# A fused attention and max-FFN kernel: later transposes go from TensorE to the DMA queue, the exp table is loaded first, and two FFN chunks are interleaved

## The chip, the cores and the metric

The kernel runs on one core of a Trainium2 chip. The metric is the device time of one execution in microseconds (us); the times below are medians over runs, and the profile is that of one further execution. In the profile the engines are PE (TensorE; PEld is its weight load), DVE (VectorE), ACT (ScalarE), POOL (GpSimd) and SP (SyncE), which here issues every DMA.

## The reference

Local attention with a few global keys feeds a feed-forward layer that takes the larger of three products:

```python
scores = scale * q @ k.T                      # (4, 8, 768, 768), head size 64
keep = (key < 8) | (0 <= query - key < 96)
scores = where(keep, scores - slope[h] * dist, -1e9)   # dist is 96 for the 8 global keys
a = softmax(scores)
x = (a @ v).transpose(0, 2, 1, 3).reshape(3072, 512)
h = max(x @ w1, x @ w2, x @ w3)               # 512 -> 768
out = h @ w_out                               # 768 -> 512
```

Inputs and output are float32; the kernel multiplies in bfloat16.

## The kernel before

The 3072 rows are cut into 24 tiles of 128, six for each of the four batches. A query tile needs its own keys, those of the tile before it and eight global keys, so that a tile's scores are two blocks of 128 keys per head. The global keys and values overwrite the first eight rows of the preceding tile's block (units G and V).

All work is written as units, and the string `SCHEDULE` names them in one order. Each engine runs its part of the units strictly in that order; waits between engines are semaphores that the framework adds. The units that matter here, with T a tile and g one of two groups of four heads:

- **L**T loads q, k and v of tile T (three DMAs of 256 KB, line 145). The last of six `raw` buffers must have been read before the load.
- **C**T.0 casts q and k to bfloat16 (`qkb`), C T.1 casts v. The last number picks the engine: 0 ACT, 1 DVE, 2 POOL, 3 half DVE and half POOL.
- **X**T turns q and k (128 rows by 1024 columns) by eight TensorE transposes (line 197) into PSUM and copies the result to `qkT` (lines 199, 200, 202).
- **S**T.g computes scores in PSUM (line 220) and ACT takes their exponential into P (line 225). A last number of 1 adds distance and mask first, by two more matmuls with `bias` (line 211); with 0, unit **M** multiplies P by `wmask` on DVE afterwards.
- **A**T.g multiplies P with v (lines 257 and 260), and DVE divides by the row sum into `xb` (lines 266 and 267).
- **T**T turns the 128 by 512 result `xb` by four TensorE transposes (line 284) and copies it to `xT` (line 285).
- **F**c.f.j is one FFN block of chunk c: four matmuls (line 296) for f of six column blocks and weight j of three; j = 0 is copied by ACT, the others are maxed in by DVE. The chunks hold 4, 2, 2, 4, 4, 4, 4 tiles, and a chunk's F units need T of all its tiles.
- **O**c.t is the second product for one tile (six matmuls, line 311), a copy and a store. **E** does this for the last chunk.
- **w**, **o** load FFN weights (512 KB each), **W**, **Q** cast them. **B** makes `bias` (line 232) and **K** makes `wmask` (line 237) for one head, both from the table of distances `rbase`.

Both X and T hold a second branch with `dma_start_transpose` on SP, reached before only for T of 99 or more, so never.

PSUM gives three buffers to FFN blocks and products (`psH`), one to transposes (`psT`), and one to each group's scores and attention product (`psS`).

Of the kernel before, what the change touches and what calls it, by code (L numbers as in the profile page):

```python
# [22 lines left out]


SCHEDULE = """
    L1 B0.1 B1.2 K0 K1 K2 K3 L2 K4 B2.2 C0.0.1 B3.2 B4.1 B5.2 X0.1 K5 K6 L3 S0.0.1 w0.0 B6.2 B7.2 S0.1.1
    G0.2 C1.0.3 X1.0 C2.0.2 C3.0.2 C0.1.1 C1.1.1 C2.1.2 M0.0 K7 M0.1 A0.0 A0.1 S1.0.1 M1.0 T0.0 S1.1.1
    A1.0 X2.3 G1.0 M1.1 A1.1 S2.0.1 L4 M2.0 w0.1 S2.1.1 T1.1 w0.2 X3.3 V1.2 A2.0 L5 M2.1 W0.0.2 C3.1.0
    A2.1 C4.0.3 G2.0 S3.0.1 S3.1.1 V2.2 T2.1 X4.3 M3.0 A3.0 M3.1 A3.1 T3.1 V3.1 G3.0 S4.0.1 W0.1.1
    S4.1.0 w1.0 G4.0 w1.1 C4.1.1 W0.2.2 F0.0.0 C5.0.2 M4.0 M4.1 F0.0.1 A4.0 A4.1 F0.0.2 X5.3 W1.0.1  # L30
    C5.1.2 F0.1.0 T4.0 W1.1.1 F0.1.1 F0.1.2 F0.2.0 V4.1 w1.2 W1.2.2 L6 w2.0 W2.0.2 C6.1.2 S5.0.0 S5.1.1
    w2.1 M5.0 F0.2.1 F0.2.2 C6.0.0 A5.0 F0.3.0 w2.2 X6.0 F0.3.1 M5.1 A5.1 S6.0.1 F0.3.2 M6.0 L7 S6.1.1
    T5.0 A6.0 W2.2.1 F0.4.0 o1 W2.1.2 L8 M6.1 A6.1 G6.0 F0.4.1 o0 o2 C7.0.2 Q1.2 F0.4.2 F0.5.0 C7.1.1
    F0.5.1 F0.5.2 C8.0.3 F1.0.0 X7.0 F1.0.1 F1.0.2 F1.1.0 L9 S7.0.0 S7.1.0 F1.1.1 F1.1.2 F1.2.0 L10 X8.0
    C8.1.0 M7.0 M7.1 F1.2.1 F1.2.2 L11 F1.3.0 G7.2 A7.0 A7.1 Q0.0 T6.1 Q2.2 L12 F1.3.1 F1.3.2 F1.4.0
    S8.0.0 S8.1.0 M8.0 T7.0 V7.1 O0.0.0 O0.1.0 C9.0.1 X9.0 M8.1 A8.0 A8.1 G8.2 F1.4.1 L13 F1.4.2 F1.5.0
    C10.0.2 T8.1 C9.1.1 C10.1.1 S9.0.0 S9.1.0 M9.0 M9.1 G9.1 O0.2.0 X10.0 F1.5.1 L14 C11.0.0 V8.1
    C12.0.2 O0.3.0 C11.1.2 A9.0 A9.1 F1.5.2 F2.0.0 X11.3 L15 S10.0.0 S10.1.0 F2.0.1 F2.0.2 C12.1.0 G10.1
    O1.0.0 M10.0 F2.1.0 M10.1 T9.0 V9.2 A10.0 F2.1.1 F2.1.2 F2.2.0 A10.1 X12.1 C13.0.2 S11.0.0 S11.1.0
    F2.2.1 O1.1.0 M11.0 M11.1 T10.0 V10.2 A11.0 F2.2.2 F2.3.0 F2.3.1 C13.1.2 A11.1 F2.3.2 X13.3 S12.0.0  # L40
    S12.1.0 F2.4.0 M12.0 M12.1 F2.4.1 F2.4.2 C14.0.0 A12.0 T11.0 F2.5.0 A12.1 F2.5.1 F2.5.2 X14.3 G12.0
    S13.0.0 M13.0 S13.1.0 F3.0.0 L16 C14.1.0 M13.1 G13.0 F3.0.1 F3.0.2 A13.0 A13.1 T12.1 F3.1.0 V13.2
    F3.1.1 C15.0.3 S14.0.0 S14.1.0 G14.0 L17 M14.0 O2.0.1 M14.1 F3.1.2 F3.2.0 C15.1.1 C16.1.1 X15.3
    A14.0 A14.1 F3.2.1 F3.2.2 T13.0 F3.3.0 L18 S15.0.0 S15.1.0 V14.1 M15.0 M15.1 C16.0.2 X16.0 F3.3.1
    O2.1.0 A15.0 A15.1 L19 L20 F3.3.2 G15.2 T14.0 C17.0.3 C18.0.1 C17.1.1 F3.4.0 S16.0.0 S16.1.0 X17.1
    V15.1 L21 L22 F3.4.1 F3.4.2 T15.0 M16.0 F3.5.0 F3.5.1 M16.1 F3.5.2 X18.0 F4.0.0 A16.0 G16.1 A16.1
    F4.0.1 F4.0.2 F4.1.0 C18.1.0 F4.1.1 S17.0.0 S17.1.0 C19.1.1 C19.0.3 C20.0.3 M17.0 L23 M17.1 V16.2
    F4.1.2 F4.2.0 F4.2.1 X19.0 A17.0 A17.1 F4.2.2 F4.3.0 F4.3.1 S18.0.0 M18.0 S18.1.0 G18.0 M18.1 O3.0.1
    O3.1.0 C21.0.3 A18.0 A18.1 X20.0 C22.0.0 C23.0.3 F4.3.2 F4.4.0 F4.4.1 S19.0.0 M19.0 S19.1.0 M19.1
    G19.2 T16.0 F4.4.2 F4.5.0 F4.5.1 A19.0 T17.0 A19.1 V19.2 C20.1.2 O3.2.1 T18.0 F4.5.2 T19.0 S20.0.0  # L50
    M20.0 S20.1.0 M20.1 O3.3.0 X21.3 F5.0.0 F5.0.1 O4.0.0 A20.0 G20.2 A20.1 V20.2 O4.1.0 S21.0.0 S21.1.0
    T20.1 M21.0 F5.0.2 X22.0 G21.1 F5.1.0 F5.1.1 F5.1.2 C21.1.0 A21.0 F5.2.0 F5.2.1 C22.1.2 F5.2.2
    F5.3.0 M21.1 F5.3.1 F5.3.2 A21.1 F5.4.0 F5.4.1 S22.0.0 S22.1.0 C23.1.2 T21.1 M22.0 F5.4.2 V21.2
    M22.1 F5.5.0 F5.5.1 X23.0 F5.5.2 A22.0 A22.1 G22.0 O4.2.0 S23.0.0 S23.1.0 T22.0 O4.3.0 O5.0.0 M23.0
    V22.2 M23.1 O5.1.0 A23.0 A23.1 O5.2.1 T23.0 O5.3.1 F6.0.0 F6.0.1 F6.0.2 F6.1.0 F6.1.1 F6.1.2 F6.2.0
    F6.2.1 F6.2.2 F6.3.0 F6.3.1 F6.3.2 F6.4.0 F6.4.1 F6.4.2 F6.5.0 F6.5.1 F6.5.2 E
"""


# [1 line left out]
def kernel(  # L61
# [77 lines left out]
    def load(T):  # L139
        b, t = divmod(T, NT)  # L140
        r = raw_pool.tile([128, 3, H, D], FP32, name="raw", tag="raw")
        raw[T] = r
        sl = slice(t * 128, (t + 1) * 128)
        for i, src in enumerate((q, k, v)):
            nc.sync.dma_start(out=r[:, i], in_=src[b, :, sl, :].rearrange("h s d -> s h d"))
# [33 lines left out]
    def early(T):  # L179
        return T < NSTART  # L180

    def u_X(T, how):
        if T >= 99:
            qkT[T] = qkT_pool.tile([128, 2, NP, 128], BF16, name="qkT", tag="qkT")
            nc.sync.dma_start_transpose(out=qkT[T].rearrange("p a j s -> p (a j) s"),
                                        in_=qb[T].rearrange("p a c -> p (a c)"))
            return
        qkT[T] = qkT_pool.tile([128, 2, NP, 128], BF16, name="qkT", tag="qkT")
        if how == 3:
            tps = [psT.tile([128, NP, 128], BF16, name="tp", tag="tp"),  # L190
                   psH.tile([128, NP, 128], BF16, name="tpk", tag="h")]
        else:
            tp = psT.tile([128, 2, NP, 128], BF16, name="tp", tag="tp")
            tps = [tp[:, a] for a in range(2)]
        for a in range(2):
            for jp in range(NP):
                nc.tensor.transpose(tps[a][:, jp], qb[T][:, a, jp * 128:(jp + 1) * 128], identb)  # L197
        if how == 3:
            nc.scalar.copy(qkT[T][:, 0], tps[0])
            nc.vector.tensor_copy(qkT[T][:, 1], tps[1])  # L200
        else:
            copies[how](qkT[T], tp)  # L202
# [25 lines left out]
    def u_B(h, how):  # L228
        g, hp = divmod(h, 4)
        j2, hh = divmod(hp, 2)  # L230
        eng = (None, nc.vector, nc.gpsimd)[how]
        eng.tensor_scalar_mul(bias[:, g, hh, j2], rbase, -slopes[h] / scale)  # L232
# [37 lines left out]
    def u_XT(T, how):  # L270
        c, i = where[T]
        if i == 0:
            xT[c] = xT_pool.tile([128, NP, len(chunks[c]) * 128], BF16, name="xT", tag="xT")
# [8 lines left out]
        x = xb[T].rearrange("p h d -> p (h d)")
        for jp in range(NP):
            nc.tensor.transpose(tp[:, jp], x[:, jp * 128:(jp + 1) * 128], identb)  # L284
        copies[how](xT[c][:, :, i * 128:(i + 1) * 128], tp)  # L285
# [85 lines left out]
    with tc.manual_schedule():  # L371
        load(0)

        make_identity(nc, identf)
# [23 lines left out]
        nc.vector.tensor_scalar_min(rbase[0:NG, 2, :], rbase[0:NG, 2, :], float(NL))  # L398
# [39 lines left out]
```

## Time and profile before

| | before |
|---|---|
| time, median of 3 runs | 195.0 us (194.93 to 195.02) |
| profiled execution | 194.84 us |
| its span (first to last instruction) | 193.1 us |
| instructions recorded | 4284 |
| read from and written to memory | 25.17 MB, 6.29 MB |
| DMA packets, of these under 512 B | 84068, 75472 |

The span starts with the first instruction that the profiler records; 1.7 us of the execution lie outside it. The packets under 512 B are those of q, k and v: a row of one head is 64 float32, 256 bytes.

### The profile page before, as it was taken

To read this page: it belongs to the slowest core of one execution; us is meant where nothing else is said; L and a number is where in the kernel's file an instruction comes from. 1 tells how busy PE (TensorE), PEld (TensorE's weight loads), DVE (VectorE), ACT (ScalarE), POOL (GpSimd) and SP (SyncE) were. 2 spreads that over 40 slices of the span, in tenths; PEclk is the share of its full clock that TensorE was granted. 3 is DMA by queue.
4 is the path that set the end of the run, shared out by engine and by line. 5 is a ranking of instruction groups with operands and counts; after the bars stand their busy time and mean duration, and the time that the engine had idled before them with its cause. 6 is when DMAs were issued, how large, how long until landed. Compare 5 with 4: busy or idle time off the path is not lost.

```text
span 193.1 us, 4284 instructions
## 1 busy us (share of the span) xinstructions
PE 178.1 (92%) x1670; PEld 103.6 (54%) x1670; DVE 124.7 (65%) x291; ACT 112.0 (58%) x176; POOL 41.1 (21%) x66
## 2 busy tenths in 40 slices
PE   0459988999999999999999999999999999999993
PEld 0236455454786678775555555555554455544442
DVE  3632577668596857878969869668555776345520
ACT  2736665664589786695567446485765276422221
POOL 6973422352320144004010230011030000000000
PEclk9999999999999999999999999999999999999999
DMA  7999999999898999999365999420220001420005
GB/s 144 218 218 259 286 213 347 237 305 259 211 257 181 233 277 232 254 262 200 100 121 139 234 218 205 98 93 3 109 112 0 2 0 58 163 109 0 3 0 217
DMA packets 84068, 31.73 MB, mean 164 GB/s; under 512 B 75472, under 2 KB 80336, under 8 KB 84048
## 3 DMA queue, kind: packets, MB, share of 16 engines
q1 hardware_dynamic: 84048, 31.46, 72.1%
q8 instruction: 13, 0.21, 0.5%
q14 instruction: 7, 0.06, 0.1%
HBM read 25.17 MB, written 6.29 MB: 163 GB/s over the span
## 4 chain that ended last, share of the span: by engine, by line
PE 88%; POOL 5%; DVE 4%; issue 1%; ACT 1%; POOLq 0%; DVEq 0%; ACTq 0%
PE h L296 48%; PE po L311 16%; PE sp L220 7%; PE tp L197 4%; POOL bias L232 4%; PE xtp L284 3%; PE sp L211 3%; PE op L257 3%; PE op L260 2%; DVE xb L267 1%; PE tpk L197 1%; ACT P L225 1%; DVE xT L285 0%; DVE qkT L200 0%; DVE rz L266 0%
## 5 line engine op out<-in xcount | busy, mean ns | idle before, releaser
L296 PE MATMUL h<-xT,w 128*128 128x512 bf16 (+1 forms) x504 | 101.8, 349 | 0.0
L296 PEld LDWEIGHTS <-w 128*128 128x128 bf16 x504 | 46.5, 98 | 37.5
L225 ACT ACTIVATE P<-sp 128x1024 bf16<-128x1024 f32 (+1 forms) x48 | 43.5, 953 | 13.3 <-PE sp L220 13.2
L301 ACT CAST h<-h 128x512 bf16<-128x512 f32 (+1 forms) x42 | 22.3, 531 | 34.9 <-PE h L296 33.7
L303 DVE TENSOR_TENSOR h<-h,h 128x512 bf16<-128x512 bf16 (+1 forms) x42 | 25.6, 609 | 19.9 <-PE h L296 19.7
L311 PE MATMUL po<-wo,ht 128*128 128x512 bf16 (+1 forms) x150 | 33.9, 371 | 0.0
L244 DVE TENSOR_TENSOR P<-P,wmask 128x1024 bf16<-128x1024 bf16 x32 | 21.9, 691 | 10.5 <-ACT P L225 10.4
L305 DVE TENSOR_TENSOR ht<-h,h 128x512 bf16<-128x512 bf16 (+1 forms) x42 | 25.6, 609 | 4.5 <-PE h L296 1.5
L267 DVE TENSOR_TENSOR xb<-op,rz 128x256 bf16<-128x256 f32 x48 | 20.4, 425 | 1.7
L311 PEld LDWEIGHTS <-ht 128*128 128x128 bf16 x150 | 13.9, 98 | 13.8
L197 PE MATMUL tp<-identb,qkb 128*128 128x128 bf16 x156 | 13.7, 231 | 6.2 <-DVE qkb L163 6.2
L197 PEld LDWEIGHTS <-qkb 128*128 128x128 bf16 x192 | 13.2, 104 | 9.4 <-DVE qkb L163 6.1
L317 ACT COPY ost<-po 128x512 f32<-128x512 f32 (+1 forms) x19 | 11.0, 582 | 11.3 <-PE po L311 10.7
L220 PEld LDWEIGHTS <-qkT 64*128 64x128 bf16 x352 | 10.2, 96 | 12.7 <-issue 7.8
L266 DVE RECIPROCAL rz<-op 128x4 f32<-128x4 f32 x48 | 8.5, 176 | 12.1 <-PE op L260 8.4
L220 PE MATMUL sp<-qkT 64*128 64x128 bf16 x352 | 16.0, 224 | 0.0
L257 PEld LDWEIGHTS <-P 128*128 128x128 bf16 x192 | 13.8, 100 | 3.5 <-DVE P L244 0.7
L257 PE MATMUL op<-va,P 128*128 128x65 bf16 x160 | 13.9, 195 | 0.9 <-DVE P L244 0.6
L202 ACT COPY qkT<-tp 128x1024 bf16<-128x1024 bf16 x12 | 12.2, 1021 | 3.8 <-PE tp L197 3.6
L285 ACT COPY xT<-xtp 128x512 bf16<-128x512 bf16 x16 | 9.5, 591 | 7.2 <-PE xtp L284 7.2
L163 POOL CAST qkb<-raw 128x1024 bf16<-128x1024 f32 x8 | 8.5, 1060 | 20.2 <-DMA raw<-in_k_dram 14.3
L177 POOL COPY va<-vaf 8x260 int32<-8x260 int32 x10 | 4.0, 398 | 40.5 <-PE op L260 40.5
(58 smaller groups left out, 140.9 us busy)
## 6 DMA issues: line engine op xcount, KB each, us to landing
raw<-in_q_dram SPq DMA_DIRECT2D x24, 256.0 KB, 5.1
raw<-in_k_dram SPq DMA_DIRECT2D x24, 256.0 KB, 5.2
raw<-in_v_dram SPq DMA_DIRECT2D x24, 256.0 KB, 5.2
out_dram<-ost SPq DMA_DIRECT2D x23, 256.0 KB, 2.1
wst<-in_moe_w_dram SPq DMA_DIRECT2D x9, 512.0 KB, 5.6
wst<-in_moe_w_out_dram SPq DMA_DIRECT2D x3, 512.0 KB, 6.1
out_dram<-ost SPq DMA_DIRECT2D x2, 128.0 KB, 1.9
```

Source lines behind the costliest of these rows:

```text
L197: nc.tensor.transpose(tps[a][:, jp], qb[T][:, a, jp * 128:(jp + 1) * 128], identb)
L202: copies[how](qkT[T], tp)
L220: nc.tensor.matmul(sp[:, hh, j2, ds], st, qkT[T][hsl, 0, jp], start=not how, stop=True, skip_group_check=True)
L225: nc.scalar.activation(P[:, :, 0:n], sp.rearrange("p a b d n -> p (a b) d n")[:, :, 0:n], AF.Exp, bias=0.0, scale=scale)
L244: nc.vector.tensor_mul(P, P, wmask[:, g, :, 0:2])
L257: nc.tensor.matmul(o, P[:, i, 0], heads(va[T])[:, h], start=True, stop=(t == 0), skip_group_check=True)
L267: nc.vector.tensor_tensor(out=x[:, 4 * g:4 * g + 4], in0=op[:, :, 0:64], in1=rz[:, :, None].to_broadcast([128, 4, D]), op=ALU.mult)
L296: nc.tensor.matmul(ps, w123[f // 2][:, dm, j, (f % 2) * 128:(f % 2) * 128 + 128], xT[c][:, dm], start=(dm == 0), stop=(dm == 3))
L301: nc.scalar.copy(h01, ps)
L303: nc.vector.tensor_max(h01s[c, f], h01s[c, f], ps)
L305: nc.vector.tensor_max(ht[c][:, f], h01s[c, f], ps)
L311: nc.tensor.matmul(po, ht[c][:, f, tt * 128:(tt + 1) * 128], wo[:, f, cols], start=(f == 0), stop=(f == NF - 1))
```

## The change

- `SCHEDULE` is another order of the same 486 units, with other engines for some. Ten of the 24 X units (tiles 13 to 15 and 17 to 23) and twelve of the 24 T units (tiles 9, 10, 12 to 14, 16 to 18 and 20 to 23) now end in 4: they take the branch with the DMA transpose, which SP issues in its queue between loads and stores.
- A 128 by 1 tile `tiny` is set to zero and put through the exponential ahead of everything else, so that ACT loads its exp table there.
- Unit B can go to ACT; of the eight, six are on DVE and two on ACT (before two on DVE and six on POOL).
- The first loads are six tiles (L0 to L5), then six FFN weights, where weights stood between tiles before. FFN blocks of chunk 0 (tiles 0 to 3) and chunk 1 (tiles 4 and 5) alternate; before, chunk 0 was finished first.
- Buffers: `cast` 3 to 4, `qkT` 4 to 5, `pp` 5 to 6.
- The exponentials with bias (last number of S is 1) are again twelve, now both groups of tiles 0 to 5.

```diff
 SCHEDULE = """
-    L1 B0.1 B1.2 K0 K1 K2 K3 L2 K4 B2.2 C0.0.1 B3.2 B4.1 B5.2 X0.1 K5 K6 L3 S0.0.1 w0.0 B6.2 B7.2 S0.1.1
+    K0 B0.1 C0.1.2 B1.1 B2.0 K1 K2 L1 B3.0 B4.1 K3 B5.1 B6.1 C0.0.1 X0.3 S0.0.1 M0.0 K4 K5 L2 B7.1
...
-    cast_pool = ctx.enter_context(tc.tile_pool(name="cast", bufs=3))
-    qkT_pool = ctx.enter_context(tc.tile_pool(name="qkT", bufs=4))
-    p_pool = ctx.enter_context(tc.tile_pool(name="pp", bufs=5))
+    cast_pool = ctx.enter_context(tc.tile_pool(name="cast", bufs=4))
+    qkT_pool = ctx.enter_context(tc.tile_pool(name="qkT", bufs=5))
+    p_pool = ctx.enter_context(tc.tile_pool(name="pp", bufs=6))
...
+    tiny = persist.tile([128, 1], FP32, name="tiny")
...
     def u_X(T, how):
-        if T >= 99:
+        if how == 4:
             qkT[T] = qkT_pool.tile([128, 2, NP, 128], BF16, name="qkT", tag="qkT")
             nc.sync.dma_start_transpose(out=qkT[T].rearrange("p a j s -> p (a j) s"),
                                         in_=qb[T].rearrange("p a c -> p (a c)"))
...
-        eng = (None, nc.vector, nc.gpsimd)[how]
-        eng.tensor_scalar_mul(bias[:, g, hh, j2], rbase, -slopes[h] / scale)
+        mul = (nc.scalar.mul, nc.vector.tensor_scalar_mul, nc.gpsimd.tensor_scalar_mul)[how]
+        mul(bias[:, g, hh, j2], rbase, -slopes[h] / scale)
...
-        if T >= 99:
+        if how == 4:
             nc.sync.dma_start_transpose(out=xT[c][:, :, i * 128:(i + 1) * 128],
                                         in_=xb[T].rearrange("p h d -> p (h d)"))
...
         load(0)
+
+        nc.vector.memset(tiny, 0.0)
+        nc.scalar.activation(tiny, tiny, AF.Exp, bias=0.0, scale=1.0)
```

**SP, the loads of the last tiles.** In the order before, from tile 19 on, SP issues nothing but loads here (three rows are one tile, `raw`):

```order
L145 DMA raw_1888<-in_q_dram 128x8x64
L145 DMA raw_1888<-in_k_dram 128x8x64
L145 DMA raw_1888<-in_v_dram 128x8x64
L145 DMA raw_1892<-in_q_dram 128x8x64
L145 DMA raw_1892<-in_k_dram 128x8x64
L145 DMA raw_1892<-in_v_dram 128x8x64
```

In the changed order, from the load of tile 19 to that of tile 20:

```order
L147 DMA raw_1998<-in_q_dram 128x8x64
L147 DMA raw_1998<-in_k_dram 128x8x64
L147 DMA raw_1998<-in_v_dram 128x8x64
L187 DMA_TRANSPOSE qkT_2026<-qkb_1955 128x8x128
L277 DMA_TRANSPOSE xT_2069<-xb_1967 128x4x128
L187 DMA_TRANSPOSE qkT_2112<-qkb_2002 128x8x128
L147 DMA raw_2121<-in_q_dram 128x8x64
L147 DMA raw_2121<-in_k_dram 128x8x64
L147 DMA raw_2121<-in_v_dram 128x8x64
```

Three transposes (q/k of tile 18, result of tile 16, q/k of tile 19) now stand between the two loads. The last reads `qkb`, a cast of the tile loaded three rows above it, so the load of tile 20 cannot be issued before tile 19 has arrived and been cast.

**ACT, the first instructions.** Before, the exp table is loaded by the first K, and no product of `bias` is on ACT:

```order
L237 ACT_TABLE_LOAD
L237 ACTIVATE wmask_103<-rbase_102 128x384 x7
L225 ACTIVATE P_195<-sp_188 128x4x128
L225 ACTIVATE P_208<-sp_201 128x4x128
L202 COPY qkT_214<-tp_215 128x1024
```

In the changed order:

```order
L377 ACT_TABLE_LOAD
L377 ACTIVATE tiny_102<-tiny_102 128x1
L239 ACTIVATE wmask_104<-rbase_103 128x384
L234 ACTIVATE bias_105<-rbase_103 128x384
L239 ACTIVATE wmask_104<-rbase_103 128x384 x2
L234 ACTIVATE bias_105<-rbase_103 128x384
L239 ACTIVATE wmask_104<-rbase_103 128x384
L201 COPY qkT_171<-tp_172 128x512
L227 ACTIVATE P_191<-sp_184 128x4x128
```

The table load has moved ahead of the wait for `rbase`, and two `bias` products stand among the first `wmask`; POOL has none left.

**ACT, where the FFN begins.** Before, the first copies of FFN blocks (`h01`) come after the exponentials of tile 4 (the first two rows); q/k of tile 5 and results of later tiles are copied between the blocks:

```order
L225 ACTIVATE P_501<-sp_490 128x1024
L225 ACTIVATE P_513<-sp_504 128x1024
L172 COPY qkT_444<-kg8_0_111 128x4x8
L301 CAST h01_528<-h_523 128x512
L199 COPY qkT_570<-tp_571 128x512
L301 CAST h01_590<-h_585 128x512
L285 COPY xT_592<-xtp_593 128x4x128
```

In the changed order they come after those of tile 5, and behind a weight cast on ACT (`w123`, unit W0.2):

```order
L227 ACTIVATE P_568<-sp_557 128x1024
L227 ACTIVATE P_581<-sp_570 128x1024
L287 COPY xT_583<-xtp_584 128x4x128
L362 CAST w123_0_114<-wst_591 128x4x256
L303 CAST h01_616<-h_611 128x512
```

The attention of one more tile lies ahead of the first FFN block, and the copy of that block waits behind the cast of a weight.

More of the change, by code (lines that the diff above doesn't have):

```diff
@@ L25 @@
 SCHEDULE = """
-    L1 B0.1 B1.2 K0 K1 K2 K3 L2 K4 B2.2 C0.0.1 B3.2 B4.1 B5.2 X0.1 K5 K6 L3 S0.0.1 w0.0 B6.2 B7.2 S0.1.1
[L27 to L55, printed above, removed]
@@ L56 @@
-    F6.2.1 F6.2.2 F6.3.0 F6.3.1 F6.3.2 F6.4.0 F6.4.1 F6.4.2 F6.5.0 F6.5.1 F6.5.2 E
+    K0 B0.1 C0.1.2 B1.1 B2.0 K1 K2 L1 B3.0 B4.1 K3 B5.1 B6.1 C0.0.1 X0.3 S0.0.1 M0.0 K4 K5 L2 B7.1
+    S0.1.1 K6 G0.0 C1.0.3 A0.0 C2.0.2 K7 X1.3 M0.1 A0.1 C1.1.0 C2.1.1 S1.0.1 S1.1.1 M1.0 L3 M1.1 A1.0
+    X2.3 A1.1 G1.0 V1.1 S2.0.1 M2.0 L4 S2.1.1 G2.0 A2.0 C3.0.2 M2.1 X3.3 L5 T0.0 A2.1 C4.0.1 S3.0.1
+    S3.1.1 T1.1 C3.1.2 V2.2 M3.0 M3.1 X4.0 A3.0 w0.0 A3.1 w0.1 G3.0 S4.0.1 S4.1.1 M4.0 M4.1 G4.2 C4.1.1
+    C5.0.1 V3.1 X5.0 T2.0 A4.0 A4.1 T3.1 S5.0.1 M5.0 S5.1.1 T4.0 M5.1 V4.2 w0.2 C5.1.2 W0.0.2 A5.0
@@ new lines @@
+    W0.1.2 W0.2.0 F0.0.0 A5.1 F0.0.1 T5.1 F0.0.2 F0.1.0 F0.1.1 w1.0 F0.1.2 F1.0.0 W1.0.2 F0.2.0 F1.0.1
+    F1.0.2 w1.2 F1.1.0 F1.1.1 w1.1 L6 W1.1.2 F1.1.2 F0.2.1 C6.0.0 F1.2.0 C6.1.1 F1.2.1 X6.1 W1.2.2
+    F1.2.2 L7 C7.0.0 F0.2.2 S6.0.0 S6.1.0 C7.1.0 M6.0 w2.2 F1.3.0 X7.0 w2.0 M6.1 W2.0.2 F1.3.1 A6.0
+    F0.3.0 w2.1 A6.1 L8 F0.3.1 G6.2 S7.0.0 S7.1.0 G7.1 C8.0.2 F1.3.2 F1.4.0 W2.1.0 M7.0 M7.1 F0.3.2
+    W2.2.0 L9 T6.1 o0 F0.4.0 C8.1.2 A7.0 A7.1 F0.4.1 X8.0 F0.4.2 F1.4.1 F1.4.2 S8.0.0 S8.1.0 T7.1 M8.0
@@ new lines @@
+    M8.1 F0.5.0 F1.5.0 F1.5.1 V7.2 o2 C9.0.2 G8.1 X9.0 o1 L10 A8.0 Q0.0 A8.1 F0.5.1 F0.5.2 Q2.2 L11
+    S9.0.0 S9.1.0 T8.0 C10.0.0 Q1.2 V8.2 F1.5.2 C9.1.2 O0.0.0 G9.2 M9.0 O0.1.0 M9.1 L12 C11.0.2 A9.0
+    X10.1 A9.1 V9.2 O0.2.0 S10.0.0 S10.1.0 G10.1 O0.3.0 T9.4 F2.0.0 C10.1.1 C11.1.0 M10.0 X11.0 C12.0.2
+    M10.1 F2.0.1 A10.0 A10.1 F2.0.2 V10.2 F2.1.0 F2.1.1 S11.0.0 S11.1.0 F2.1.2 F2.2.0 C12.1.0 M11.0
+    M11.1 F2.2.1 F2.2.2 T10.4 X12.1 L13 C13.0.2 A11.0 O1.0.0 A11.1 F2.3.0 L14 X13.4 F2.3.1 F2.3.2
@@ new lines @@
+    S12.0.0 S12.1.0 M12.0 M12.1 T11.1 F2.4.0 O1.1.0 F2.4.1 F2.4.2 F2.5.0 F2.5.1 F2.5.2 F3.0.0 A12.0
+    F3.0.1 A12.1 C14.0.2 L15 C13.1.2 F3.0.2 X14.4 G12.2 F3.1.0 C14.1.0 F3.1.1 S13.0.0 M13.0 S13.1.0
+    G13.1 L16 O2.0.0 M13.1 C15.0.1 F3.1.2 F3.2.0 A13.0 A13.1 F3.2.1 V13.2 F3.2.2 S14.0.0 X15.4 S14.1.0
+    G14.2 T12.4 M14.0 F3.3.0 C16.0.3 M14.1 F3.3.1 L17 F3.3.2 A14.0 F3.4.0 A14.1 V14.2 X16.3 F3.4.1 T13.4
+    S15.0.0 M15.0 S15.1.0 C15.1.2 O2.1.0 M15.1 F3.4.2 F3.5.0 A15.0 A15.1 F3.5.1 F3.5.2 T14.4 L18 C17.0.0
@@ new lines @@
+    C16.1.2 C17.1.2 G15.0 S16.0.0 M16.0 S16.1.0 X17.4 M16.1 T15.1 O3.0.0 O3.1.0 O3.2.1 F4.0.0 C18.0.1
+    V15.2 A16.0 C18.1.2 A16.1 V16.1 G16.2 F4.0.1 F4.0.2 L19 C19.0.2 S17.0.0 S17.1.0 X18.4 M17.0 M17.1
+    F4.1.0 F4.1.1 A17.0 F4.1.2 F4.2.0 T16.4 C19.1.2 A17.1 F4.2.1 F4.2.2 S18.0.0 M18.0 S18.1.0 M18.1
+    X19.4 F4.3.0 L20 L21 C20.0.0 T17.4 X20.4 G18.0 C20.1.2 F4.3.1 F4.3.2 A18.0 A18.1 T18.4 F4.4.0 F4.4.1
+    S19.0.0 S19.1.0 F4.4.2 M19.0 F4.5.0 M19.1 F4.5.1 C21.0.0 X21.4 L22 L23 F4.5.2 A19.0 A19.1 V19.2
@@ new lines @@
+    O3.3.0 O4.0.0 G19.1 T19.0 O4.1.1 S20.0.0 S20.1.0 F5.0.0 M20.0 M20.1 F5.0.1 G20.1 C22.0.0 F5.0.2
+    A20.0 F5.1.0 A20.1 V20.2 F5.1.1 F5.1.2 S21.0.0 S21.1.0 C21.1.2 M21.0 M21.1 C23.0.3 F5.2.0 G21.1
+    F5.2.1 F5.2.2 X22.4 F5.3.0 A21.0 A21.1 V21.2 F5.3.1 F5.3.2 S22.0.0 S22.1.0 M22.0 F5.4.0 M22.1 T20.4
+    T21.4 F5.4.1 C22.1.2 A22.0 G22.0 F5.4.2 F5.5.0 A22.1 X23.4 F5.5.1 F5.5.2 T22.4 S23.0.0 S23.1.0
+    O4.2.0 V22.1 C23.1.2 M23.0 M23.1 O4.3.1 A23.0 A23.1 T23.4 O5.0.0 O5.1.0 O5.2.0 O5.3.1 F6.0.0 F6.0.1
@@ L57 @@
+    F6.0.2 F6.1.0 F6.1.1 F6.1.2 F6.2.0 F6.2.1 F6.2.2 F6.3.0 F6.3.1 F6.3.2 F6.4.0 F6.4.1 F6.4.2 F6.5.0
+    F6.5.1 F6.5.2 E
 """
```

## The prediction, made before the changed kernel was run

> **What bounds the kernel now.** I read the page first: busy time, the span in 40 slices (4.83 us each) and the shares of the chain that ended last.
>
> ```profile
> PE 178.1 (92%) x1670; PEld 103.6 (54%) x1670; DVE 124.7 (65%) x291; ACT 112.0 (58%) x176; POOL 41.1 (21%) x66
> PE   0459988999999999999999999999999999999993
> DMA  7999999999898999999365999420220001420005
> GB/s 144 218 218 259 286 213 347 237 305 259 211 257 181 233 277 232 254 262 200 100 121 139 234 218 205 98 93 3 109 112 0 2 0 58 163 109 0 3 0 217
> PE 88%; POOL 5%; DVE 4%; issue 1%; ACT 1%; POOLq 0%; DVEq 0%; ACTq 0%
> ```
>
> PE is full from the eighth slice on, and the chain runs through it for 88% of the span. The rest of the chain is a start in which PE waits. The DMA engines are full until about 90 us and mostly free behind 120 us. So three things count: PE work, PE's idle time at the start, and whether loads keep pace in the first half. The stages, in the view of busy time by stretch (stretch, length, then busy us of each engine; at the end clock, DMA share, GB/s):
>
> ```profile
> 31.40:58.00 26.60, 26.59 (x257) 16.43 (x256) 19.73 (x46) 16.21 (x26) 8.13 (x9) 1.00 1.08 260
> 87.00:123.00 36.00, 35.97 (x335) 19.49 (x334) 29.48 (x66) 21.64 (x33) 5.29 (x9) 1.00 0.89 173
> 123.00:169.00 46.00, 46.00 (x402) 24.68 (x401) 29.14 (x62) 26.84 (x41) 4.31 (x10) 1.00 0.15 58
> ```
>
> PE has no gap to speak of in any of them, at full granted clock; no other engine passes 82%. But a busy PE is not PE's price for an instruction, since matmuls overlap. The price is the time between one group and the next in the chain of waits (start, length, what):
>
> ```profile
> 31.41 0.86 PE h L296 x4
> 50.12 0.45 PE tp L197 x8
> 52.05 0.55 PE sp L220 x16
> 54.47 1.31 PE h L296 x12
> 56.26 0.22 PE xtp L284 x4
> 66.57 1.29 PE po L311 x6
> 124.93 0.26 PE op L257 x8
> 19.34 0.43 PE sp L211 x2
> 184.55 5.21 PE po L311 x30
> 189.84 0.42 DVE ost L317
> ```
>
> So X on TensorE costs 0.45 us, T 0.22, an FFN block 0.86 (0.44 in a chunk of two tiles), a tile's scores 0.55 for both groups, `bias` 0.43 a group, an attention product 0.26, O 1.29. Over all units of the table this makes 168.5 us: FFN 93.3, O and E 31.0, X 10.8, T 5.3, scores and `bias` 16.7, attention 11.4. The last matmul ends at 189.8, so PE idles 21.3 us in all. Where?
>
> ```profile
> 3.73 1.28 ACT L237 ACT_TABLE_LOAD   x1 [3.73 <-DVE rbase L398]
> 3.83 4.99 POOL bias L232 x4
> 8.88 1.24 POOL bias L232
> 10.20 1.23 POOL bias L232
> 11.47 0.37 PE sp L211
> 12.21 0.60 ACT L225 ACTIVATE P<-sp 128x512 bf16<-128x512 f32 x1 [3.14 <-PE sp L220]
> 30.99 0.20 PE op L257
> ```
>
> Six `bias` products on POOL hold the second group of tile 0 until 11.47; ACT idles 3.14 us for it. From there tiles follow one another until 30.99, when the attention of tile 4 begins; behind that PE is full. Ahead of 30.99 PE has done X for five tiles (2.25), scores and `bias` of tiles 0 to 4 (5.9), attention of tiles 0 to 3 (1.8), four T (0.9) and two FFN blocks (1.7): 12.6 us. So **18.4 us of the idle time lie ahead of 30.99**, 2.9 behind it.
>
> **The change, part by part.** *Transposes leave PE.* Ten X by 0.45 and twelve T by 0.22 are 4.5 + 2.6 = **7.1 us** of PE work gone. All lie behind tile 9, where PE is full, so all of it counts if PE stays the bound. Their copies go too:
>
> ```profile
> L202 ACT COPY qkT<-tp 128x1024 bf16<-128x1024 bf16 x12 | 12.2, 1021 | 3.8 <-PE tp L197 3.6
> L285 ACT COPY xT<-xtp 128x512 bf16<-128x512 bf16 x16 | 9.5, 591 | 7.2 <-PE xtp L284 7.2
> ```
>
> ACT loses six of the first and eleven of the second kind, some 12 us; three more q/k casts and three weight casts there (1.07 each) give back 6. DVE sheds five splits of casts and copies. None of this was the bound: nothing is added for it.
>
> *What a DMA transpose costs* the trace does not show. Nearest rows:
>
> ```profile
> 113.31 1.14 SPq L145 DMA_DIRECT2D raw<-in_k_dram  x1
> 114.49 1.10 SPq L145 DMA_DIRECT2D raw<-in_v_dram  x1
> raw<-in_k_dram SPq DMA_DIRECT2D x24, 256.0 KB, 5.2
> out_dram<-ost SPq DMA_DIRECT2D x23, 256.0 KB, 2.1
> ```
>
> With the queue full, 256 KB in packets of 256 B (1024 of them, 64 per DMA engine) pass in 1.14 us; a store into a free queue has landed in 2.1. An X transpose is 256 KB whose contiguous block rows are 256 B too. Call its time in the queue c (T: half). From the load row by size of piece: c is 1.14 for 256 B, 2.3 for 128 B, 4.6 for 64 B, 9.1 for 32 B. Below, a queue that overlaps it wholly gives 0. I take 1.14, the load's row, as nearest in bytes and packets, and keep 0 to 9.1.
>
> What decides is the tightest stretch. It runs from the end of O3.2 (chunk 3's third product) to S of tile 22. In it PE has 30 FFN blocks (25.9), three O (3.9), scores of five tiles (2.75), six attentions (3.1) and a T (0.2): 35.9 us. Ahead of tile 22's transpose the queue carries, with it, 0.9 for the last store's copy, 15 loads by 1.14 (17.1), three stores by 0.9 (2.7), five X (5c) and three T (1.5c). 20.7 + 6.5c = 35.9 gives **c = 2.3**. Below that, transposes cost nothing; above, each us of c costs 6.5 us. Single steps also hold at c = 1.14: the last T has the four O of chunk 5 (5.2 us) ahead of chunk 6, against 0.8 for DVE, 0.6 in the queue and about 2 to land. SP waits in line here: each transpose waits for its cast or division, and the next tile's load stands behind it. Loads behind 123 us have a DMA share of 0.15 to fill, so later loads are bearable. I charge **0**; at c = 9.1 it is the last but one of the rivals.
>
> The Trainium skill speaks against this step: "VectorE: DVE Perf Modes", section "The three transpose paths", gives 1309 ns for a 128 by 128 DMA transpose and 390 ns on TensorE. Its TensorE figure does not agree with the 56 ns apiece of the chain (0.45 / 8); no run here shows its DMA figure. If eight blocks went one by one, c would be 10.5 (estimate from that page) and the sum as in the rival of the swamped queue. Its page "Advanced Engine Details and Errata", section "X-Bar Transpose (TRN2)", says the opposite, 350 to 400 GB/s, an estimated c of 0.7, with which the sum is my forecast.
>
> *The start.* `bias` goes to DVE and ACT, and ACT's table load hides in the wait for `rbase`:
>
> ```profile
> L232 DVE TENSOR_SCALAR bias<-rbase 128x384 bf16<-128x384 f32 x2 | 1.0, 503 | 0.0
> L225 ACT ACTIVATE P<-sp 128x1024 bf16<-128x1024 f32 x40 | 38.9, 1024 | 7.9 <-PE sp L220 7.8
> 16.09 1.04 POOL L163 CAST qkb<-raw 128x1024 bf16<-128x1024 f32 x1 [2.60 <-DMA raw<-in_k_dram]
> L363 ACT CAST wo<-wst 128x1024 bf16<-128x1024 f32 x1 | 1.1, 1078 | 0.0
> L301 ACT CAST h<-h 128x512 bf16<-128x512 f32 x30 | 17.7, 591 | 30.2 <-PE h L296 29.0 <-DVE ht L305 1.1
> ```
>
> Five products by 0.5 on DVE end near 6.2, so tile 0 is through by about 11 and loads become the pace. Tile 3's k has landed at 16.09. Seven more loads at 1.19 (issue to issue in the rows above) end tile 5's at 24.4. Three weights of 0.52 MB at 264 GB/s (mean of slices 5 to 12) take 2.0 each: 30.4. The third is cast on ACT (1.08), behind it ACT copies the first FFN block (0.59), and only then is its PSUM buffer free for the fourth: 32.1. ACT's own work fits: from 8.0 (X of tile 0) about 21 us of exponentials, copies and `wmask`, so it would be through by 29.4 without a wait. By 32.1 PE has done X and scores of six tiles (2.7 + 7.7), their attention (2.9), six T (1.3) and three blocks (2.6): 17.2. Idle: 14.9 instead of 18.4, **a gain of 3.5**. Bounds: fourth block at 30 (5.6) and no gain (35.6).
>
> *Loads in the first half.* K of tile 10 has 14.7 MB in and ahead of it; at 246 GB/s (mean of the first 12 slices) it lands at about 61, and the ACT cast adds 1.1. PE reaches X10 after 46.4 us of work plus 14.9 idle, 61.3: about 1 us of wait, **1.5** with what tiles 7 and 8 may add. Bounds 0 and 5. Alternating two FFN chunks changes no PE work; it asks less weight per us, which I count as cover for this term. More `cast`, `qkT` and `pp` buffers only remove waits.
>
> *Sum*, for the profiled execution: 193.1 - 7.1 - 3.5 + 1.5 + 0 = 184.0 of span, with the 1.74 outside it 185.7. The median stands 0.16 above that execution: **185.9**.
>
> **Rivals.** *The start gains nothing* (ACT or the weights hold the fourth block until 35.6, or loads cost 5): 189.4, with both 192.9. For it: ACT's 21 us leave little slack, and the DMA share there is already above 1. Against: the `bias` chain of 7.6 us is plainly gone.
>
> *The transposes become the bound, slower.* One mechanism: SP's one queue. With pieces of 64 B c is 4.6, and from O3.2 on each us above 2.3 costs 6.5: 185.9 + 15 = 201. It crosses 195.0 at c = 3.7. For it: two-byte elements must be scattered, and 22 transposes stand ahead of loads. Against: twice the load's packet cost is still free.
>
> *The transposes swamp the queue.* c of 9.1: behind tile 13's load 10 X and 12 T are 16c = 146 us, with 11 loads of 3.4 (37) and some 15 stores (14) from about 70: 267, then chunk 6 and the end (24): about 290. By the skill's 1309 ns it would be about 313 (estimate).
>
> *The moved transposes are not missed* because another wait (the casts that X waits for, or later loads) takes their place: the 7.1 are lost and the result is 193, or 195 when late loads add 2.
>
> **Chances.** Forecast (182 to 189): 0.56. Start gains nothing, loads cost more, or the 7.1 us are not missed (189 to 193): 0.13. Transposes or late loads eat nearly all (193 to 194.6): 0.05. No change, within 0.2%, about what a measurement of this kernel can tell from none: 0.04. Slower through the queue, 195.4 to 212: 0.16. Swamped: 0.06. So faster 0.74, same 0.04, slower 0.22. The range 182 to 200 holds the first four and the lower part of the fifth, about 0.83; its low end is the early fourth block (2.1 less) without load waits (1.5 less).
>
> **What would show it.** In the changed profile: 128 fewer matmuls on PE, at 56 ns apiece; first PE wait for `bias` gone, PE full by 32 instead of 31 but with tile 5 behind it; a queue time per transpose near that of a load; PE's idle time near 19. I am wrong if transposes land much later than loads, if S or F wait for SP's queue late in the span, or if loads behind transposes starve a cast.

## The result: 186.0 us after 195.0, as forecast

The changed kernel takes 186.03 us (median of 4 runs, 185.20 to 186.62) against 195.01; the ratio is 0.953, with a 95% interval of 0.949 to 0.957. The profiled execution took 185.96 us, its span is 184.2 us; the forecast was 185.9 and 184.0. Medians and differences below leave out four executions that took over 1.5% longer than the fastest of the same kernel: one of four in e2, two of ten in e6 and one of the kernel before.

The page after the change, in the rows shown of before (busy time, slices of 4.6 us, shares of the chain that ended last):

```profile
PE 169.5 (92%) x1542; PEld 94.3 (51%) x1542; DVE 119.0 (65%) x277; ACT 104.8 (57%) x161; POOL 37.6 (20%) x65
PE   0678689999899999999999999998999999999992
DMA  6999999999799999999999899999899232610006
PE 69%; SPq 13%; DMA 10%; POOL 2%; issue 1%; ACT 1%; DVE 1%; DVEq 0%; ACTq 0%
```

PE has 128 fewer matmuls and 8.6 us less busy time. DMA is now full until about 143 us (31 slices), where it was full until 90. And the chain is no longer PE alone: SP's queue and DMA hold 23% of it. Some 37 of these 42 us lie ahead of 47 us, in the loads of tiles and weights at the start; behind that the chain passes through them once, from 116.7 to 123 us, by the issue of a transpose and the loads behind it. The same three stages, by busy time per stretch:

```profile
32.00:58.00 26.00, 25.14 (x247) 16.33 (x245) 19.03 (x44) 16.74 (x26) 7.30 (x9) 1.00 1.03 258
87.00:123.00 36.00, 36.00 (x320) 18.37 (x320) 28.50 (x61) 18.07 (x27) 6.56 (x12) 1.00 1.09 209
123.00:160.00 37.00, 36.43 (x303) 18.17 (x298) 24.52 (x53) 20.82 (x30) 4.11 (x8) 1.00 0.76 162
```

PE is still full, but from 87 to 123 us the DMA share is 1.09 (it adds up the times of packets, which overlap where it passes 1): two bounds lie on top of each other. The transposes themselves, first in SP's part of the timeline (start, length of the issue on SP, what), then among the DMA issues (median to landing):

```profile
112.30 2.12 SPq L187 DMA_TRANSPOSE qkT<-qkb  x1
114.52 1.21 SPq L277 DMA_TRANSPOSE xT<-xb  x1
115.91 1.23 SPq L187 DMA_TRANSPOSE qkT<-qkb  x1
117.20 0.57 SPq L147 DMA_DIRECT2D raw<-in_q_dram  x1
```

```profile
q1 hardware_dynamic: 101136, 35.66, 88.5%
xT<-xb SPq DMA_TRANSPOSE x12, 2.7
qkT<-qkb SPq DMA_TRANSPOSE x10, 4.4
```

The queue's packets took 88.5% of 184.2 us, 163.0, against 72.1% of 193.1, 139.2. The 23.8 us more, over ten transposes of 256 KB and twelve of half, make c = 1.5 us (23.8 / 16). Against e8 below, which has the loads of this order and no DMA transpose (68.7% of 197.5 us, 135.7), it is 1.7. The forecast took 1.14. The Trainium skill, "VectorE: DVE Perf Modes", section "The three transpose paths", gives 1309 ns for a 128 by 128 block; taken one after another (an estimate of 10.5 us for eight) that is not what these rows show: eight blocks landed 4.4 us after their issue, queue included. Another page of the Trainium skill, "Advanced Engine Details and Errata", section "X-Bar Transpose (TRN2)", with transposes as fast as other DMAs, is nearer: 5.7 us of queue time per MB here, against 4.4 for all transfers before (139.2 us for 31.7 MB).

The start, in PE's and ACT's timeline (start, length, engine, line, what, and in brackets the idle time before and what ended it):

```profile
29.29 1.02 PE L298 MATMUL h<-xT,w 128*128 128x512 bf16 x4
30.40 1.02 PE L298 MATMUL h<-xT,w 128*128 128x512 bf16 x4
31.64 8.85 PE L298 MATMUL h<-xT,w 128*128 128x512 bf16 x56
```

```profile
29.79 0.59 ACT L287 COPY xT<-xtp 128x512 bf16<-128x512 bf16 x1
30.54 1.05 ACT L362 CAST w<-wst 128x1024 bf16<-128x1024 f32 x1 [0.16 <-DMA wst<-in_moe_w_dram]
31.49 0.58 ACT L303 CAST h<-h 128x512 bf16<-128x512 f32 x1
```

The third block starts at 31.64, when the cast of its weight on ACT has ended (31.59), and the fourth 0.86 later, at 32.5 (forecast 32.1). The cast was foreseen as what paces this place. The copy behind it, which the forecast had just ahead of the fourth block, ended at 32.07 and held nothing.

### The profile page after: what moved, and what is told of

The parts are those of the page before. It is cut to its first block, busy times and chain, and to the rows that moved or that the text cites. A ratio compares the mean times of both kernels' runs of the same rounds, so it can differ in the third digit from the quotient of the medians.

```text
span 184.2 us, 4060 instructions
## 1 busy us (share of the span) xinstructions
PE 169.5 (92%) x1542; PEld 94.3 (51%) x1542; DVE 119.0 (65%) x277; ACT 104.8 (57%) x161; POOL 37.6 (20%) x65
## 3 DMA queue, kind: packets, MB, share of 16 engines
q1 hardware_dynamic: 101136, 35.66, 88.5%
## 4 chain that ended last, share of the span: by engine, by line
PE 69%; SPq 13%; DMA 10%; POOL 2%; issue 1%; ACT 1%; DVE 1%; DVEq 0%; ACTq 0%
PE h L298 40%; PE po L313 17%; SPq L147 13%; DMA raw<-in_k_dram 6%; PE sp L222 4%; DMA wst<-in_moe_w_dram 4%; PE op L259 2%; PE op L262 2%; PE tp L199 2%; POOL w L362 1%; ACT P L227 1%; PE xtp L286 1%; SPq L352 1%; POOL va L156 1%; DVE qkb L165 0%
## 5 line engine op out<-in xcount | busy, mean ns | idle before, releaser
L313 PE MATMUL po<-wo,ht 128*128 128x512 bf16 (+1 forms) x150 | 33.4, 371 | 0.0
L246 DVE TENSOR_TENSOR P<-P,wmask 128x1024 bf16<-128x1024 bf16 x30 | 21.4, 721 | 7.6 <-ACT P L227 7.1
L313 PEld LDWEIGHTS <-ht 128*128 128x128 bf16 x150 | 14.0, 98 | 14.4 <-issue 0.2
L222 PEld LDWEIGHTS <-qkT 64*128 64x128 bf16 x352 | 10.0, 94 | 12.8 <-issue 7.3
L259 PEld LDWEIGHTS <-P 128*128 128x128 bf16 x192 | 13.5, 99 | 5.0 <-ACT P L227 1.5
L222 PE MATMUL sp<-qkT 64*128 64x128 bf16 x352 | 15.3, 219 | 0.7 <-ACT qkT L201 0.6
L165 POOL CAST qkb<-raw 128x1024 bf16<-128x1024 f32 x9 | 9.4, 1040 | 30.1 <-DMA raw<-in_k_dram 30.1
L199 PE MATMUL tp<-identb,qkb 128*128 128x128 bf16 x92 | 7.9, 227 | 7.8 <-DVE qkb L165 7.4
L259 PE MATMUL op<-va,P 128*128 128x65 bf16 x160 | 13.7, 193 | 0.7 <-ACT P L227 0.7
L199 PEld LDWEIGHTS <-qkb 128*128 128x128 bf16 x112 | 7.3, 104 | 9.1 <-DVE qkb L165 7.6
L262 PEld LDWEIGHTS <-P 128*128 128x128 bf16 x160 | 10.8, 97 | 1.9
L319 DVE COPY ost<-po 128x512 f32<-128x512 f32 (+1 forms) x5 | 3.2, 639 | 12.3 <-PE po L313 12.3
L262 PE MATMUL op<-va,P 128*128 128x65 bf16 x128 | 11.1, 193 | 0.0
```

The lines of the kernel that those rows point to most:

```text
L222: nc.tensor.matmul(sp[:, hh, j2, ds], st, qkT[T][hsl, 0, jp], start=not how, stop=True, skip_group_check=True)
L246: nc.vector.tensor_mul(P, P, wmask[:, g, :, 0:2])
L259: nc.tensor.matmul(o, P[:, i, 0], heads(va[T])[:, h], start=True, stop=(t == 0), skip_group_check=True)
L262: nc.tensor.matmul(o, P[:, i, 1], heads(va[T - 1])[:, h], start=False, stop=True, skip_group_check=True)
L313: nc.tensor.matmul(po, ht[c][:, f, tt * 128:(tt + 1) * 128], wo[:, f, cols], start=(f == 0), stop=(f == NF - 1))
```

## The experiments

The differences below are to the changed kernel's 186.03 us unless another is named. The runs of the kernel before beside them had medians of 194.95 to 195.10.

### e1, e2 and e8: transposes back on TensorE

In e1 all 22 go back to TensorE in the places that they have in the changed order, in e2 only the twelve of results, in e8 all, but spread out.

```diff
-X13.4 ... X23.4      T9.4 ... T23.4        (changed)
+X13.3 X14.3 X15.3 X17.1 X18.0 X19.0 X20.0 X21.3 X22.0 X23.0      (e1, e8)
+T9.0 T10.0 T12.1 T13.0 T14.0 T16.0 T17.0 T18.0 T20.1 T21.1 T22.0 T23.0      (e1, e2, e8)
```

> The changed kernel with all 22 DMA transposes put back on TensorE, with the copies on the engines that each had before. Theory (the transposes counted as PE work: ten by 0.45 and twelve by 0.22): 7.1 us slower than the changed kernel, 193.1 (192 to 194.2), and the DMA share falls by some 24 us of queue time. Rival 1, the freed queue gives part back since loads and stores no longer stand behind transposes: at most 4 slower, 190 or less. Rival 2, the copies on ACT and DVE count as well: 9 or more slower, 195 or more.

> The changed kernel with the twelve transposes of attention results back on TensorE; those of q/k stay in the DMA queue. Theory (PE work only, the parts add): 12 by 0.22, 2.6 us slower, 188.6 (188 to 189.5). Rival, a DMA transpose of a result lands late for its FFN chunk, so that PE gains little by it: no more than 1 slower.

> The changed kernel with all 22 transposes on TensorE as in e1, but each placed apart from its neighbours in the order: q/k some three FFN blocks behind their cast and about four ahead of their scores, results three blocks behind their attention. Theory (e1's 24 us are waits of PE in its fixed order, beside 7.1 of work): well below e1, 193 to 199. Rival 1, TensorE transposes cost PE far more than 0.45 and 0.22 in this order: 205 or more, as e1. Rival 2, only the work is left: 193.1 within 0.7.

Measured: e1 210.43 us (24.4 slower; ratio to before 1.078, 1.072 to 1.085), e2 199.01 (13.0 slower; 1.017, 1.012 to 1.022), e8 199.38 (13.4 slower; 1.024, 1.020 to 1.027). For e1 and e2 the theory of bare PE work fell by far. Busy time per stretch in e1:

```profile
58.00:87.00 29.00, 26.63 (x286) 18.17 (x289) 20.35 (x47) 18.60 (x31) 9.86 (x13) 1.00 0.93 210
87.00:123.00 36.00, 31.68 (x272) 16.94 (x276) 21.92 (x48) 17.64 (x26) 4.77 (x10) 0.91 0.51 110
123.00:160.00 37.00, 32.45 (x287) 17.11 (x290) 22.06 (x48) 21.86 (x31) 4.18 (x7) 1.00 0.62 133
```

In e1 PE is not busy for 11.2 us from 58 to 160 (some 2 of them are ten matmul records that are missing beside the weight loads), where the changed kernel has 0.6, and its clock is 0.91 in one stage. What PE waited for (waiter, what for, us in total, times, longest), first in e1, then in e8:

```profile
PE tp L199 <- ACT xT L287: 3.4, 3, 1.5
PE xtp L286 <- DVE xT L287: 1.7, 1, 1.7
PE xtp L286 <- DVE qkT L204: 1.7, 1, 1.7
PE xtp L286 <- DVE xb L269: 2.4, 4, 1.1
```

```profile
PE tp L198 <- ACT xT L286: 4.1, 4, 1.6
PE tp L198 <- DVE xT L286: 1.2, 1, 1.2
```

The changed order puts a transpose next to its cast or division, which a DMA issued by SP can wait for beside PE; on PE itself the whole engine stands (the last row of e1, 2.4 us). But the larger wait is another: transposes stood until the copy of an earlier one had emptied the one PSUM buffer that transposes share (`psT`), 6.8 us in the first three rows. A DMA transpose uses neither PE nor that buffer. The waits of PE that the profile lists sum to 24.4 us in e1 and to 11.2 in the changed kernel. The 13.2 more, 7.1 of work and some 3 of clock (0.09 of 36 us) make 23.5 us, and e1 is 24.4 slower. The number lies in the range of its Rival 2, and the copies do count, though as waits for a buffer and not as time of ACT and DVE.

In e2 PE's waits sum to 19.5 us; the 8.3 more, 2.6 of work and some 2 of clock (0.95 in the 37 us from 123 to 160) make 12.8 of 13.0. With the transposes spread (e8) they sum to 15.8, of which 5.3 are for `psT` again; the 4.6 more and 7.1 of work are 11.7 of 13.4. So e8, 0.4 above the range of its theory, is consistent with the 7.1, but does not measure it by itself. What the other 1.7 us of e8 are stays open.

### e7 and e12: a few transposes moved in the kernel before

Here the order of before stays. e7 moves the transposes of tiles 20 to 23; e12 gives it the buffers and leaves the last result on TensorE. Times are against the kernel before.

```diff
-X20.0 X21.3 X22.0 X23.0      T20.1 T21.1 T22.0 T23.0
+X20.4 X21.4 X22.4 X23.4      T20.4 T21.4 T22.4 T23.4        (e7; e12 has T23.0)
-cast_pool bufs=3, qkT_pool bufs=4
+cast_pool bufs=4, qkT_pool bufs=5        (e12)
-        if T >= 99:
+        if how == 4:
```

> The kernel before, its own order, with only the last four q/k transposes and the last four of results (tiles 20 to 23) in the DMA queue, which is mostly free there. Theory (PE work, nothing else): 4 by 0.45 and 4 by 0.22, 2.7 us faster than before, 192.3 (191.8 to 192.8). Rival 1, the transposes land late for an order that was made for TensorE: no gain, 195 or more. Rival 2, the copies that go with them count too: 4 or more faster.

Measured: 197.65 us, **slower** than before (ratio 1.010, 1.007 to 1.013), as Rival 1 has it. DVE's timeline and, for PE, the row of who waited for whom (waiter, what for, us in total, times, longest) in e7:

```profile
129.51 0.43 DVE L160 CAST qkb<-raw 128x512 bf16<-128x512 f32 x1 [3.02 <-DMA qkT<-qkb]
```

```profile
PE h L296 <- DMA xT<-xb: 2.4, 1, 2.4
```

The cast of a later tile waited 3.0 us for the third cast buffer, which a transpose in the queue still read; DVE's FFN work stood behind that cast, and PE stood 0.85 us behind DVE for it. The last chunk waited 2.4 us for its last result. For PE that is 3.3 us against 2.7 us of work saved. The execution that was profiled took 195.95 us, 1.1 more than the profiled one of the kernel before and near the lowest of the ten (195.83 to 198.17), so that these waits explain it only roughly; what the longer ones spent 2 us more on, no trace shows.

> The kernel before with the q/k transposes of tiles 20 to 23 and the results of 20 to 22 in the DMA queue, as in e7, but a fourth cast buffer and a fifth qkT buffer, and the last result on TensorE. In e7 DVE waited 3.0 us for a cast buffer that a DMA transpose still read, and the last chunk 2.4 us for its last result. Theory (those two waits hid the gain): 4 by 0.45 and 3 by 0.22, 2.5 us faster than before, 192.6 (192 to 193.3). Rival, other waits in SP's queue take their place: 194.5 or more.

Measured: 193.11 us (ratio 0.989, 0.988 to 0.991), 2.1 us faster than before with an interval of 1.7 to 2.4, where 2.46 of PE work left. In e12 PE has no gap from 87 to 169 us:

```profile
87.00:123.00 36.00, 35.96 (x336) 19.45 (x335) 29.93 (x66) 21.64 (x33) 4.90 (x9) 1.00 0.96 181
123.00:169.00 46.00, 46.00 (x370) 23.38 (x369) 29.24 (x61) 23.76 (x37) 4.56 (x10) 1.00 0.38 102
```

Seven transposes off PE are thus worth nearly their price in the chain, in a kernel where neither the cast buffer nor the last result has to wait. e12 changes three things against e7 (two buffers and the last result) and was not split further; what the buffers alone would bring to the kernel before was not run.

### e3 to e6: transposes issued a second and a third time

Each extra transpose reads the same source into a scratch tile that nobody reads.

```diff
             nc.sync.dma_start_transpose(out=qkT[T].rearrange("p a j s -> p (a j) s"),
                                         in_=qb[T].rearrange("p a c -> p (a c)"))
+            d = dup_pool.tile([128, 8, 128], BF16, name="dup", tag="dup")
+            nc.sync.dma_start_transpose(out=d, in_=qb[T].rearrange("p a c -> p (a c)"))
```

> The changed kernel with each DMA transpose issued twice, the second into a scratch tile that nobody reads. By the DMA shares of the two profiles one q/k transpose takes about 1.5 us of queue time, so twice is 3.0. Theory of the prediction (free up to 2.3, then 6.5 us per us): 4.6 slower, 190.6 (188.5 to 193). Rival 1, the queue still has room because SP runs ahead of its need: within 1 of the changed kernel. Rival 2, the queue is already full from tile 13 on and pays in full, 16 by 1.5: 20 or more slower.

> The changed kernel with each DMA transpose issued three times, two of them into scratch tiles that nobody reads: about 4.5 us of queue time for one of q/k. Theory of the prediction (6.5 us for each us above 2.3): 14 slower, 200 (196 to 204). Rival 1, the queue has room: within 3. Rival 2, the queue pays in full for what exceeds its free time (32 by 1.5 is 48 more, some 16 us were free): 30 slower, 216.

> The changed kernel with only its ten q/k transposes (256 KB) issued a second time into scratch tiles. All 22 twice cost 23.1 us, about in full. Theory 1, the DMA engines' time is what is paid (by bytes, 10 of 16 parts): 14.5 slower than the changed kernel, 200.5. Theory 2, SP's issue is what is paid (1.25 us for each transpose in the trace, whatever its size, 10 of 22 parts): 10.5 slower, 196.5. The prediction's own rule (free up to 2.3 us a transpose): at most 4 slower.

> The changed kernel with only its twelve transposes of attention results (128 KB) issued a second time into scratch tiles. Theory 1, DMA engines' time (6 of 16 parts): 8.7 slower than the changed kernel, 194.7. Theory 2, SP's issue (12 of 22 parts): 12.6 slower, 198.6. The prediction's own rule: at most 4 slower.

Measured: e3 209.17 us (23.1 slower), e4 234.75 (48.7), e5 196.15 (10.1), e6 195.99 (10.0). The prediction's own rule fell in all four. Rival 2 of e3 held (20 or more); that of e4, 216, was exceeded by 19 us. There is no free room for ten more transposes, the fewest that were tried. Per extra transpose it is 1.05 us in e3, 1.16 for the third in e4, 1.01 in e5 and 0.83 in e6. The 256 KB ones cost a fifth more than those of half the size, which speaks against bytes as the price: Theory 2 of e5 fits (10.5), and e6 lies between its two theories (8.7 and 12.6). It does not single out the issue on SP, which takes 1.2 us for either, since the time of the queue's packets does not go by bytes either: it is 17.6 us more than in the changed kernel in e5 (93.1% of 194.0) and 14.9 more in e6 (91.3% of 194.9). Stretches of e3:

```profile
87.00:123.00 36.00, 29.16 (x250) 14.72 (x256) 21.05 (x45) 16.34 (x23) 6.19 (x13) 0.94 1.08 205
123.00:160.00 37.00, 29.38 (x214) 14.04 (x217) 18.14 (x40) 14.34 (x22) 3.62 (x6) 0.87 1.01 184
```

PE is not busy for 14.5 us in these two (some 2.6 of them are twelve missing matmul records) and its clock is below 1, so part of each price is clock, not waiting. DMA is full as well, at 1.0 to 1.1. What reaches PE is late q/k, a wait that the changed kernel does not have (2.6 us in e5, 4.1 in e6):

```profile
PE sp L226 <- DMA qkT<-qkb: 9.6, 5, 2.4
```

Whether SP's issue or the DMA engines alone would set the time is not settled by these rows.

### e9 and e10: parts of the start

e9 puts `bias` back (two products on DVE, six on POOL) and drops the early exponential; e10 runs the blocks of chunk 0 ahead of those of chunk 1.

```diff
-B0.1 B1.1 B2.0 B3.0 B4.1 B5.1 B6.1 B7.1        (changed)
+B0.1 B1.2 B2.2 B3.2 B4.1 B5.2 B6.2 B7.2        (e9)
-        nc.scalar.activation(tiny, tiny, AF.Exp, bias=0.0, scale=1.0)
...
-F0.0.0 ... F0.1.2 F1.0.0 F0.2.0 F1.0.1 F1.0.2 F1.1.0 ... F1.5.2        (changed)
+F0.0.0 ... F0.5.2 F1.0.0 ... F1.5.2        (e10)
```

> The changed kernel with the eight bias products on the engines of before (six on POOL) and without the early exp table load; loads and order stay. Theory 1 (in the changed trace the start is paced by loads, tile 4 waits for its k until 20.9 us): no more than 1 slower, 186 to 187. Theory 2 (the prediction's reading, the bias chain held the start): all of the 3.1 us that PE's idle time ahead of the FFN fell are lost, 188.5 to 190.

> The changed kernel with the FFN blocks of chunks 0 and 1 in sequence, chunk 0 first, in the same places of the order or as soon after as their weights are cast; loads stay. Theory 1 (the alternation bridges the wait for the third pair of weights, which is cast at 47.9 us): chunk 0 reaches its fifth block near 42 and waits, 4 to 6 slower, 190 to 192. Theory 2 (attention units fill the gap, alternation is free but brings nothing): 186 to 187.

Measured: e9 189.45 us (3.4 slower; ratio to before 0.971, 0.968 to 0.974): Theory 2. POOL's timeline in e9:

```profile
6.54 0.61 POOL L156 CAST vaf<-raw 128x512 bf16<-128x512 f32 x1 [3.47 <-DMA raw<-in_v_dram]
7.12 7.28 POOL L234 TENSOR_SCALAR bias<-rbase 128x384 bf16<-128x384 f32 x6
```

The products stand behind a cast of v that waits for its load, so they end at 14.4, three us later than in the kernel before. PE waits 5.8 us for them in four waits; in the kernel before it was 3.0, in the changed kernel nothing. e9 therefore shows that `bias` on POOL holds the start in this order, but is a harder test than the kernel before was. The table load, which e9 moves back as well, held nothing there: ACT waited 4.2 us for scores soon after it. Its first FFN block starts at 33.58 instead of 29.29, though loads were issued as early.

e10: 198.32 us (12.3 slower; ratio to before 1.016, 1.012 to 1.019), far beyond both theories. PE's timeline and a stretch of e10:

```profile
47.09 1.89 PE L298 MATMUL h<-xT,w 128*128 128x512 bf16 x4 [2.85 <-POOL w L362]
53.66 9.39 PE L298 MATMUL h<-xT,w 128*128 128x512 bf16 x48 [2.56 <-ACT w L362]
```

```profile
32.00:58.00 26.00, 18.84 (x112) 8.72 (x111) 12.19 (x24) 11.78 (x16) 5.79 (x7) 0.80 1.06 260
```

The wait for weights is as Theory 1 has it (2.9 and 2.6 us), but PE idles 7.2 us in this stretch against 0.9 in the changed kernel, and its clock is 0.80 where that has 1.00. Four matmuls took 1.89 us (1.02 in the changed kernel's row above). The queue loses time too: from 58 to 87 us the DMA share is 0.61, in the changed kernel 1.04. How the 12.3 us divide between these was not taken apart.

### e11: ACT issues the transposes

```diff
-            nc.sync.dma_start_transpose(
+            nc.scalar.dma_start_transpose(        (both branches)
```

> The changed kernel with the 22 DMA transposes issued by ACT in place of SP. Theory 1 (SP's 1.25 us of issue for each transpose is what is paid at the edge): loads go out earlier, faster by 1 to 3, 183 to 185. Theory 2 (the DMA engines' time is what is paid): 185 to 187. Rival, ACT's own work stands behind 22 waits and 27 us of issue: 190 or more.

Measured: 193.94 us (7.9 slower; ratio to before 0.994, 0.990 to 0.998): the rival. ACT's timeline, with its queue's issues:

```profile
77.36 1.62 ACTq L187 DMA_TRANSPOSE qkT<-qkb  x1
79.03 1.09 ACT L227 ACTIVATE P<-sp 128x512 bf16<-128x512 f32 x2 [2.81 <-issue]
```

An exponential whose scores had ended at 77.0 stood behind the issue of a transpose. That is not the larger part of the loss, though. PE's waits sum to 16.9 us, 5.7 more than in the changed kernel, and most of that is transposed q/k that arrived late (2.1 us more were for copies on ACT):

```profile
PE sp L222 <- DMA qkT<-qkb: 5.4, 4, 2.2
```

A transpose now waits its turn on ACT, and lands a median of 5.0 us (result) and 5.5 us (q/k) after its issue instead of 2.7 and 4.4. What SP would gain can't be read from this run, since this loss covers it. No run beat the changed kernel.

## Why the prediction was right, and where its reasons were not

**PE is the bound and a transpose costs it 0.45 or 0.22 us (7.1 off).** Right. The chain of the changed kernel has the same prices. By them PE's work is 161.4 us after the change; its last matmul ends at 180.8, so PE idles 19.4 us, as forecast (14.9 ahead of the fourth block, 4.4 behind). That is bookkeeping, since the 7.1 are already in the 161.4. e12 measures the price most directly: 2.1 us (1.7 to 2.4) for 2.46.

**The start (3.5 off).** Right in size: PE's idle time ahead of the fourth block is 32.5 - 17.2 = 15.3 against 18.4, so 3.1. By the forecast's own numbers the third block, which needs the weight cast itself, would have ended at 32.3, behind the copy at 32.1; that step was left out, and 32.5 is what came. The cause was named rightly: with `bias` on POOL again e9 loses 3.4, in a harder test. My later reading, that loads would hide it (Theory 1 of e9), was the wrong one.

**Loads in the first half (1.5 on).** The sum is right: 4.1 us idle behind the fourth block, forecast 4.4. Most of this is no gap: PE is not busy for 1.5 us between 32.5 and 180.9, and in the kernel before for 0.5 us where the prices gave 2.9. So the prices leave out some 2.5 us of work in both kernels, and the term itself came out at 1.0 to 1.2. The two largest gaps are 0.85 us for a weight cast that ended at 47.9 and 0.6 us behind 123 us, the latter at the end of the way through a transpose's issue and the load of k behind it. But I called the alternation of the two chunks a cover for this term and gave it no price; without it the kernel loses 12.3 (e10). In this order the term was small because of the alternation.

**Transposes in the queue (0 on).** Right for the kernel as it is, by a wrong argument, and so in part by luck. The step that failed is the threshold: "Below that, transposes cost nothing", with c = 2.3 and 6.5 us for each us above. It counted one late stretch with an empty queue at its beginning, and by queue time alone. The runs show a queue with little or nothing to spare: at c = 1.5 PE and DMA are both full, and ten or more further transposes cost about 1.0 us each (e3 to e6), by number more than by size. So the slower rivals were nearer than I put them: doubling the transposes, to a c of 3.0, cost 23 us (e3) where the rule gave 4.6.

**That the order can be judged apart from the transposes.** I did not say it, but the sum treats them so. e1 and e7 speak against it: moved back in place they cost 24 us instead of 7, and eight of them put into the old order cost some 2 us (ratio 1.010) instead of gaining 2.7. The gain belongs to transposes, places and buffers together.

## What to carry to other kernels

When work moves from a full engine to a queue, price it by the chain of waits, then look for what its latency holds: the buffer it reads, the next load behind it, the last step of a chunk. One more buffer of two kinds, and the last step left on PE, turned a loss into nearly the full gain (e7, e12). Look too for what the full engine gives back beside its work: here the one PSUM buffer of transposes (e1). A kernel at the edge of two bounds hides it well: double the moved work once, and see whether it was free.
